# Moving the weight rounding to an even rhythm, the packed scores one step later, and computing the router's logits with the router's weights held still in four column groups

## The chip, the cores and the metric

The kernel runs on one core of one Trainium2 chip. The metric is the device time of one execution in microseconds; the time before is the median of three runs. The engines are named as the profile names them: PE is TensorE (PEld its weight loads), ACT is ScalarE, DVE is VectorE, POOL is GpSimd, SP is SyncE, which issues nearly all of the DMAs.

## The reference

```python
# packed attention, 8 batches x 8 heads, 576 tokens, 32 packed queries, head size 64
p_packed = sm_attn(p, k, v)
out = sm_attn(q, p_packed, p_packed)
# a dense layer on the 4608 tokens of width 512, inner width 2048
h = x @ w_in; x = (h * sigmoid(h)) @ w_out
# a router with 8 experts, one expert per token, inner width 1024
logits = x @ w_gate; e_idx = argmax(logits); gate_w = softmax(logits)[e_idx]
eom = sigmoid(x @ w_output_gate)[e_idx]
out = gate_w * eom * (relu(x @ w1[e_idx]) @ w2[e_idx])
```

## The kernel before

Batches 0 to 7 run one after the other in the function batch. Each has 16 steps f, one for each 128 of the 2048 inner columns of the dense layer. A step issues on PE, in this order: mm1 (12 matmuls of 288 columns, into the two banks of the PSUM tile h, of which there is one), whatever the schedule names for position 0 of the step, mm2 of two steps earlier (12 matmuls of 512 columns into four accumulators acc0 to acc3), and what the schedule names for position 1. On ACT and DVE it issues the gate: ACT's tanh reads h (L658), DVE's product reads h (L659), ACT rounds to the high half ghi (L664), DVE subtracts for the low half glo (L669); the last 64 tokens have halves of their own (gl). The next mm1 may start when L659 is done with h.

The order of the instructions on each engine is the program's (the schedule is written out by hand); semaphores come from the tile framework, which follows who uses which tile.

Work that rides along in these steps:

- The attention of the next batch, s1 to s9. s1(0) and s1(1) are the scores of the packed queries with the two halves k0 and k1 of the keys. They write the shared PSUM tile of pool ps_a (there is one, too); DVE takes the maximum (L535) and ACT copies the scores to e (L536). After s1(1), two exponentials (L542) run on ACT in the next step, and s2(0), at position 1 of step 4, transposes their first half.
- step_m at position 0 of the even steps: the fused query weights of two of the next steps, 16 matmuls of 64x32 tiles into ps_a.
- The rows of the batch before. At step 1 the last mm2 of batch b-1 is issued; ACT then moves the four accumulators out (evac, L711). Where b is even, a fifth accumulator, accL, follows at once in the place of acc3 (48 matmuls). row_t transposes two blocks of 128 tokens at steps 3 and 7, row_logits takes their logits at steps 5 and 9 (where b is even a single fifth block follows at 11 and 13). finish finds the experts, place counts and scatters the tokens' numbers into the tables perm (POOL, indirect DMA) at step 11 or 15, and the rows go to memory as xr (SP).
- split_slot, in batches 1 to 6: ACT rounds a raw piece of the expert weights (512 KB) to a tile shi, of which there are two (L478), DVE subtracts (L479), the next step stores both parts (ws, L466 and L467), and the slot itself issues the load of a later piece. There are 64 pieces; slots are the steps with f % 3 < 2, ahead of mm2 in the program. SP works its list in order, so a DMA that has to wait holds up those behind it.

row_logits holds 128 tokens as weights for each of four slices of 128 features and moves the 8 router columns past them: 8 matmuls for a pair of blocks, each of two fp32 instructions. In the last batch's tail (last_rows) the same is done between blocks of the accL matmuls. After batch 7 the experts run in tiles of 128 tokens.

Of the kernel before, what the change touches and what calls it, by code (L numbers as in the profile page):

```python
# [8 lines left out]
F32 = mybir.dt.float32  # L9
F32R = mybir.dt.float32r  # L10
# [3 lines left out]
ALU = mybir.AluOpType  # L14
# [5 lines left out]
B, H, S, D = 8, 8, 576, 64  # L20
# [3 lines left out]
NF = FF // 128  # L24
E8 = 8
# [5 lines left out]
XW = DM + 1  # L31
SCALE = 1.0 / 8.0

C_ID, C_E, C_OFF, C_LT, C_J, C_END = 0, 128, 136, 144, 208, 209
HS = S // 2
EARLY = 3
NSTATIC = NBLK + 2
# [3 lines left out]
def constants():  # L41
    p = np.arange(128)
    c = np.zeros((128, C_END), np.float32)
    c[:, C_ID:C_ID + 128] = np.eye(128)
    e = np.arange(E8)
    c[:, C_E:C_E + E8] = e
    c[:, C_OFF:C_OFF + E8] = (e - E8) * CAP
    c[:, C_LT:C_LT + E8 * E8] = (e[None, :] < e[:, None]).reshape(1, -1)
    c[:, C_J] = p
    k = np.full((128, 256), 0x3F80, np.uint16)  # L50
    k[:, :128] *= p[:, None] < p[None, :]
    t = np.stack([block_tokens(i) for i in range(NBLK)], axis=1).astype(np.int32)
    t[:, np.arange(NBLK) % NPERM > 0] -= NTOK
    return {"cst": c, "cstk": k, "cstt": t}
# [25 lines left out]
class Kernel:  # L80
# [12 lines left out]
    def run(self):  # L93
        tc, nc = self.tc, self.nc
# [21 lines left out]
        self.flip = False  # L116
        self.ppt, self.m, self.g, self.loads = {}, {}, {}, {}
        self.graws = []
        self.wgt = cp.tile([128, 4, E8], F32, name="wgt")
        self.tok = self.rt.tile([128, NBLK], I32, name="tok")  # L120
        self.w_in = self.pin.tile([128, 4, FF], F32, name="w_in")
        self.a1 = [self.pa.tile([128, 5, 128], F32, name="a1t")]
# [96 lines left out]
    def last_rows(self):  # L219
        b = B - 1  # L220
        self.mm2(b, NF - 2)
        hi, lo = self.g.pop((b, NF - 1))
        g = self.rows_group(b, range(4))
        for j in (3, 0, 1, 2):
            self.mm2_block(self.acc[j], hi[:, j * 128:j * 128 + 128], lo[:, j * 128:j * 128 + 128], NF - 1, False, True)
        for j in (3, 0, 1, 2):
            self.evac(g, j, self.acc[j])
        acc = self.ps_acc.tile([128, 512], F32, tag="acc3", name="accL")
        side = {2: lambda: self.row_t(g, 3, 0), 5: lambda: self.row_logits(g, 3, 0),
                6: lambda: self.row_t(g, 1, 2), 9: lambda: self.row_logits(g, 1, 2),  # L230
                12: lambda: self.place(g)}
        for ff in range(NF):
            self.mm2_block(acc, self.gl[0][:, ff, :], self.gl[1][:, ff, :], ff, ff == 0, ff == NF - 1)
            if ff in side:
                side[ff]()
            run(self.late)
        self.group_l = self.rows_group(b, [4], g)
        self.evac(self.group_l, 4, acc)
# [17 lines left out]
            g["t"][j] = t  # L256

    def row_logits(self, g, *js):
        ps = self.ps_a.tile([128, 2, 512], F32, tag="a", name="ps_rl")
        for n, j in enumerate(js):  # L260
            for k in range(4):
                self.nc.tensor.matmul(ps[:, 0, n * E8:n * E8 + E8], g["t"][j][:, k * 128:k * 128 + 128], self.wgt[:, k, :],
                                      start=(k == 0), stop=(k == 3))
        for n, j in enumerate(js):
            g["left"] -= 1
            self.nc.vector.tensor_copy(out=g["lg"][:, g["at"][j], :], in_=ps[:, 0, n * E8:n * E8 + E8])
        if not g["left"]:
            self.finish(g)

# [64 lines left out]
    def batch(self, b, hook=None):  # L334
        sched = self.extra_steps(b)
        for f in range(NF):
            s = b * NF + f
            self.split_store()
            self.mm1(b, f)
            self.fill(b, 1, True)  # L340
            self.act(b, f)
            run(sched.get((f, 0), []))
            self.split_hi(b, f)
            self.split_lo(b, f)
            wait = f < 2 and b % 2 == 0 and b > 0
            self.graws = [*self.graws[-1:], self.graw]
            if not wait:
                self.split_left(b, f, self.graw)
            run(self.late)
            if 0 < b < B - 1 and f % 3 < 2:  # L350
                self.split_slot()
            self.fill(b, 2 if f < 2 else 1)
            if s > 1:
                self.mm2(*divmod(s - 2, NF))
            if wait and f == 1:
                for i in range(2):
                    self.split_left(b, i, self.graws[i])
            run(sched.get((f, 1), []))
            if hook:
                hook(f)  # L360
            if b == 0 and f == 8:
                self.a2[1] = [self.p1.tile([128, 2, S], F32R, tag=f"a2_1{i}", name="a2") for i in range(2)]
            if b == 0 and f == 4:
                self.setup_late()
            if b == 0 and f == 0:
                t = self.rt.tile([128, 4, 512, 2], U32, tag="wg", name="stg4")
                for i in range(4):
                    self.f64_load(t[:, i], True)
            if b == 0 and f == 14:
                self.mid = self.rt.tile([128, E8 * DM], F32, tag="wg", name="mid")  # L370
                self.nc.sync.dma_start(self.wgt, self.i["wgt"])

    def fill(self, b, conv, defer=False):
        if b == 0:
# [2 lines left out]
    def extra_steps(self, b):  # L377
        sched = {}

        def at(f, pos, fn):  # L380
            sched.setdefault((f, pos), []).append(fn)

        if b + 1 < B:
            att = self.att_steps(b + 1)
            for f, pos, *step in ((0, 1, "s1", 0), (2, 1, "s1", 1), (4, 1, "s2", 0), (5, 1, "s3", 0), (6, 1, "s2", 1),
                                  (7, 1, "s3", 1), (8, 1, "s4"), (9, 1, "s5", 0), (10, 0, "s6", 0), (10, 1, "s7", 0),
                                  (11, 1, "s8", 0), (11, 1, "s9", 0), (12, 1, "s5", 1), (13, 0, "s6", 1), (13, 1, "s7", 1), (14, 1, "s8", 1), (14, 1, "s9", 1)):
                at(f, pos, att[tuple(step)])
            for f, what in ((0, "k1"), (2, "q0"), (5, "v1"), (9, "q1")):
                at(f, 1, lambda what=what: self.load_att(b + 1, what))  # L390
            at(14, 0, lambda: self.step_m(b + 1, 0))
        if b + 2 < B:
            for what in ("p", "k0", "v0"):
                at(13, 0, lambda what=what: self.load_att(b + 2, what))
        if b > 0:
            js = [(3, 0), (1, 2)] + ([(4,)] if b % 2 == 0 else [])
            for n, r in enumerate(js):
                at(4 * n + 3, 0, lambda r=r: self.row_t(self.group, *r))
                at(4 * n + 5, 0, lambda r=r: self.row_logits(self.group, *r))
            at(4 * len(js) + 3, 0, lambda: self.place(self.group))  # L400
        for c in range(1, 8):
            at(2 * c - 2 + (b == 0 and (c == 1 or c % 2 == 0)), 0, lambda c=c: self.step_m(b, c))
        return sched
# [65 lines left out]

    def split_slot(self):  # L470
        nc = self.nc
        if not self.split_raw:
            self.split_raw = [self.mid[:, k * 1024:k * 1024 + 1024] for k in (1, 2, 3)]
            self.split_raw += [self.stg.tile([128, 1024], F32, name="sw")]
        if len(self.split_loaded) == 2 or not self.split_jobs:
            for w, dst in self.split_loaded[:1]:
                hi = self.stg.tile([128, 1024], F32R, tag="shi", bufs=2, name="shi")
                nc.scalar.copy(out=hi, in_=w)  # L478
                nc.vector.tensor_tensor(out=w.bitcast(F32R), in0=w, in1=hi.bitcast(F32), op=ALU.subtract)  # L479
                self.split_done.append((w, hi, dst))  # L480
            self.split_loaded = self.split_loaded[1:]
        if self.split_jobs:
            which, e, k = self.split_jobs.pop(0)
            w = self.split_raw[self.split_n % 4]
            self.split_n += 1
            if which == 1:
                nc.sync.dma_start(w, self.i["w1"][e].rearrange("(k p) f -> p k f", p=128)[:, k, :])
                dst = self.ws1[e, k]
            else:
                nc.sync.dma_start(w.rearrange("p (k d) -> p k d", k=2),  # L490
                                  self.i["w2"][e].rearrange("(k p) d -> p k d", p=128)[:, 2 * k:2 * k + 2, :])
                dst = self.ws2[e, k]
            self.split_loaded.append((w, dst))


    def load_att(self, b, what, dst=None):
# [206 lines left out]
    def rows_group(self, b, js, rest=None):  # L703
# [1 line left out]
        n = len(js)  # L705
        return {"n": n, "left": n, "b": b, "js": js, "at": {j: k for k, j in enumerate(js)}, "t": {},
                "xr": rt.tile([128, 5, XW], F32, tag="xr", name="xr") if rest is None else rest["xr"][:, 4:5],
                "lg": rt.tile([128, 5, E8], F32, tag="lg", bufs=2, name="lg")}

    def evac(self, g, j, acc):  # L710
        self.nc.scalar.activation(out=g["xr"][:, g["at"][j], :DM], in_=acc, func=AF.Copy, scale=0.5)  # L711
# [323 lines left out]
```

## Time and profile before

| what | value |
|---|---|
| median of three runs | 1384.9 us (1384.56 to 1385.53) |
| the profiled execution | 1384.82 us, its span 1383.1 us |
| mean granted TensorE clock | 0.969 |
| PE busy | 1279.1 us, 92% |
| DVE, ACT, POOL busy | 652.3, 506.6, 172.8 us |
| DMA | 238.56 MB, mean 172 GB/s |

A busy share is a mean over stages with different limits. The clock is the share of 2.4 GHz that was granted; 0.5 is 1.2 GHz. An arrow in a row names what ended the idle time before an instruction.

### The profile page before, as it was taken

Reading aid. Unit: us, or ns where it says so; the run is one execution under the profiler, and the core shown is the slowest. Engines: PE = TensorE matmul, PEld = TensorE weight load, DVE = VectorE, ACT = ScalarE, POOL = GpSimd, SP = SyncE. Lnnn points to the kernel's source line nnn. Section 1 sums busy time; section 2 is a strip of 40 time slices with the busy share of each in tenths; the row PEclk is TensorE's granted clock in tenths of the full one; section 3 lists DMA queues with packets and bytes.
Section 4 is the critical chain, followed back from the end, with each engine's and each line's share of the span. In section 5 each row is a group of like instructions: output and inputs, shape, how many; then the busy total and the mean of one; then the engine's idle time right before and its main releaser. Section 6 shows DMA issues by size and latency. Waiting matters only on the chain. (4 is left out here: it accounts for less than half of the span.)

```text
span 1383.1 us, 24453 instructions
## 1 busy us (share of the span) xinstructions
PE 1279.1 (92%) x8414; PEld 1024.6 (74%) x8416; DVE 652.3 (47%) x1417; ACT 506.6 (37%) x980; POOL 172.8 (12%) x236
## 2 busy tenths in 40 slices
PE   6776999799799899899899999969999999999997
PEld 3555787687587687687687888748888888888886
DVE  6979558257557356657356644311222222222221
ACT  3323544354454354454354433212232222222222
POOL 0324101000101000101000111111122122112210
PEclk9899999999899999999999999989999999999999
DMA  8553259665977755987955317651555473822630
GB/s 293 195 171 109 79 203 172 236 234 201 198 251 171 237 192 194 253 246 161 246 190 185 100 31 151 108 124 47 191 191 199 156 269 109 293 63 70 222 137 22
DMA packets 110623, 238.56 MB, mean 172 GB/s; under 512 B 30753, under 2 KB 48929, under 8 KB 110498
## 3 DMA queue, kind: packets, MB, share of 16 engines
q1 hardware_dynamic: 103266, 217.46, 53.0%
q0 software_dynamic: 7232, 19.44, 4.1%
q8 instruction: 77, 1.26, 0.4%
q14 instruction: 48, 0.39, 0.1%
HBM read 401.91 MB, written 87.14 MB: 354 GB/s over the span
## 5 line engine op out<-in xcount | busy, mean ns | idle before, releaser
L700 PE MATMUL acc<-wo,ghi 128*128 128x512 f32 x1024 | 320.4, 394 | 0.0
L700 PEld LDWEIGHTS acc<-wo,ghi 128*128 128x128 f32 x1024 | 194.5, 190 | 38.7
L649 PE MATMUL ps_h<-a,m_hi 128*128 128x288 f32 x1024 | 213.7, 301 | 0.8 <-DVE a L615 0.8
L700 PE MATMUL acc<-wo,glo 128*128 128x512 f32 x512 | 212.5, 415 | 0.6 <-ACT xr L711 0.6
L992 PE MATMUL py<-queue_q_buf,hhi 128*128 x608 | 191.9, 397 | 0.0
L649 PE MATMUL ps_h<-a,m_lo 128*128 128x288 f32 x512 | 162.9, 318 | 24.0 <-DVE g L659 20.9
L964 PE MATMUL pu<-queue_q_buf,xhi 128*128 x560 | 175.9, 395 | 0.0
L978 DVE TENSOR_TENSOR hlo<-ph,hhi 128x512 fp32r<-128x512 f32 x76 | 49.0, 686 | 263.1 <-ACT hhi L977 152.7
L649 PEld LDWEIGHTS ps_h<-a,m_hi 128*128 128x128 f32 x1024 | 169.6, 194 | 2.6 <-DVE a L615 1.0
L659 DVE SCALAR_TENSOR_TENSOR g<-g,ps_h 128x576 f32<-128x576 f32 x128 | 96.1, 751 | 132.0 <-ACT g L658 131.6
L658 ACT ACTIVATE g<-ps_h 128x576 f32<-128x576 f32 x128 | 83.3, 651 | 157.8 <-PE ps_h L649 153.3
L649 PEld LDWEIGHTS ps_h<-a,m_lo 128*128 128x128 f32 x512 | 99.1, 194 | 51.2 <-DVE g L659 30.2
L992 PE MATMUL py<-queue_q_buf,hlo 128*128 x304 | 123.7, 407 | 13.4 <-DMA xix_p<-perm 13.4
L992 PEld LDWEIGHTS py<-queue_q_buf,hhi 128*128 128x128 f32 x608 | 115.4, 190 | 25.6
L700 PEld LDWEIGHTS acc<-wo,glo 128*128 128x128 f32 x512 | 97.4, 190 | 43.3 <-issue 25.0
L767 POOL DMA_INDIRECT perm<-tok,dsti x36 | 38.5, 1069 | 682.8 <-DVE dsti L764 649.6
L964 PEld LDWEIGHTS pu<-queue_q_buf,xhi 128*128 128x128 f32 x560 | 105.2, 188 | 23.8
L664 ACT CAST ghi<-g 128x512 fp32r<-128x512 f32 x128 | 79.3, 620 | 106.5 <-DVE g L659 104.4
L964 PE MATMUL pu<-queue_q_buf,xlo 128*128 x280 | 114.3, 408 | 0.2 <-ACT hs L966 0.2
L966 ACT ACTIVATE hs<-pu 128x512 f32<-128x512 f32 x76 | 45.4, 598 | 166.4 <-PE pu L964 158.1
L669 DVE TENSOR_TENSOR glo<-g,ghi 128x512 fp32r<-128x512 f32 x128 | 88.5, 691 | 31.4 <-ACT ghi L664 26.7
L997 POOL DMA_INDIRECT out<-y,xix x38 | 38.3, 1009 | 335.1 <-ACT y L995 330.2
(183 smaller groups left out, 1513.8 us busy)
## 6 DMA issues: line engine op xcount, KB each, us to landing
queue_q_buf<-ws SPq DMA_DIRECT2D x70, 4096.0 KB
ws<-shi SPq DMA_DIRECT2D x64, 512.0 KB
mid<-in_w SPq DMA_DIRECT2D x48, 512.0 KB
ws<-mid SPq DMA_DIRECT2D x48, 512.0 KB
att_v<-in_v SPq DMA_DIRECT2D x15, 640.0 KB
og<-in_wog SPq DMA_DIRECT2D x35, 256.0 KB
att_k<-in_k SPq DMA_DIRECT2D x15, 576.0 KB
xr<-xr SPq DMA_DIRECT2D x32, 256.5 KB
```

What stands on the lines that cost most here:

```text
L649: nc.tensor.matmul(ps[:, hf, :288], lw[:, qd, fs], rx[:, qd, ts], start=(i == 0), stop=(i == 5))
L658: nc.scalar.activation(out=g2, in_=ps[:, :, :288], func=AF.Tanh, scale=0.5)
L659: nc.vector.scalar_tensor_tensor(out=g2, in0=g2, scalar=1.0, in1=ps[:, :, :288], op0=ALU.add, op1=ALU.mult)
L664: self.nc.scalar.copy(out=hi, in_=self.graw[:, :512])
L669: self.nc.vector.tensor_tensor(out=lo, in0=self.graw[:, :512], in1=self.ghi.bitcast(F32), op=ALU.subtract)
L700: self.nc.tensor.matmul(acc, l, r, start=(first and i == 0), stop=(last and i == 2))
L767: nc.gpsimd.indirect_dma_start(out=self.perm[(i0 + r) % NPERM], out_offset=bass.IndirectOffsetOnAxis(ap=di[:, r:r + 1], axis=0), in_=self. ...
L964: nc.tensor.matmul(ps, l[:, ks], w[:, k, r, ns], start=(i == 0), stop=(i == 11))
L966: nc.scalar.activation(out=self.hs[j][:, n * 512:n * 512 + 512], in_=ps, func=AF.Relu)
L978: nc.vector.tensor_tensor(out=lo[:, n], in0=ps, in1=hi[:, n].bitcast(F32), op=ALU.subtract)
L992: nc.tensor.matmul(ps, l[:, k // 4, ks], w[:, k // 2, r, (k % 2) * DM:(k % 2) * DM + DM], start=(i == 0), stop=(i == 23))
L997: nc.gpsimd.indirect_dma_start(out=self.out, out_offset=bass.IndirectOffsetOnAxis(ap=ix[:, 0:1], axis=0), in_=y, in_offset=None, bounds_ch ...
```

## The change

Six edits: a slot is a step with (s - 16) % 3 < 2 where s counts through the batches, so the rhythm doesn't start anew in each batch; at step 1 the slot comes after mm2, the evacuation and accL; two pieces are loaded at the end of batch 0, so every slot rounds one piece and loads one; s1(1) and the load of q0 move from step 2 to step 3; a pair's logits are computed with 32 columns of router weights held still in one of four column groups, 128 tokens moving, into four partial results that ACT copies to SBUF, and one step later one matmul with a 0/1 matrix sums them and turns them back; lg has one buffer in place of two.

```diff
-C_ID, C_E, C_OFF, C_LT, C_J, C_END = 0, 128, 136, 144, 208, 209
+C_ID, C_E, C_OFF, C_LT, C_J, C_SEL, C_END = 0, 128, 136, 144, 208, 209, 225
+    n = np.arange(2 * E8)
+    c[:, C_SEL:] = (p[:, None] % 32 == n % E8) & (p[:, None] // 32 % 2 == n // E8)
...
-        side = {2: lambda: self.row_t(g, 3, 0), 5: lambda: self.row_logits(g, 3, 0),
-                6: lambda: self.row_t(g, 1, 2), 9: lambda: self.row_logits(g, 1, 2),
+        side = {2: lambda: self.row_t(g, 3, 0), 4: lambda: self.row_logits(g, 3, 0), 5: lambda: self.row_logits2(g, (3, 0)),
+                6: lambda: self.row_t(g, 1, 2), 8: lambda: self.row_logits(g, 1, 2), 9: lambda: self.row_logits2(g, (1, 2)),
...
     def row_logits(self, g, *js):
...
+        for k in (0, 2, 1, 3):
+            for n, j in enumerate(js):
+                c = 2 * (k // 2) + n
+                nc.tensor.matmul(ps[32 * c:32 * c + 32, 0, :128], self.wgt[:, k * E8:k * E8 + 32], g["t"][j][:, k * 128:k * 128 + 128],
+                                 start=(k % 2 == 0), stop=(k % 2 == 1))
+        g["part"] = g["t"][js[1]][:, :128]
+        nc.scalar.copy(out=g["part"], in_=ps[:, 0, :128])
+
+    def row_logits2(self, g, js, h=None):
+        ps = (self.ps_a.tile([128, 2, 512], F32, tag="a", name="ps_rl") if h is None else h)[:, 0, 288:288 + 2 * E8]
+        self.nc.tensor.matmul(ps, g["part"], self.cst[:, C_SEL:C_SEL + 2 * E8], start=True, stop=True)
+        self.row_logits_out(g, ps, js)
...
-            if 0 < b < B - 1 and f % 3 < 2:
+            slot = 0 < b < B - 1 and (s - NF) % 3 < 2
+            if slot and f != 1:
                 self.split_slot()
             self.fill(b, 2 if f < 2 else 1)
             if s > 1:
                 self.mm2(*divmod(s - 2, NF))
+            if slot and f == 1:
+                self.split_slot()
...
+            if b == 0 and f == 15:
+                self.split_load()
+                self.split_load()
...
-            for f, pos, *step in ((0, 1, "s1", 0), (2, 1, "s1", 1), (4, 1, "s2", 0), (5, 1, "s3", 0), (6, 1, "s2", 1),
+            for f, pos, *step in ((0, 1, "s1", 0), (3, 1, "s1", 1), (4, 1, "s2", 0), (5, 1, "s3", 0), (6, 1, "s2", 1),
...
-            for f, what in ((0, "k1"), (2, "q0"), (5, "v1"), (9, "q1")):
+            for f, what in ((0, "k1"), (3, "q0"), (5, "v1"), (9, "q1")):
...
                 at(4 * n + 5, 0, lambda r=r: self.row_logits(self.group, *r))
+                if len(r) == 2:
+                    at(4 * n + 6, 0, lambda r=r: self.row_logits2(self.group, r, self.h))
...
     def split_slot(self):
         nc = self.nc
...
+        for w, dst in self.split_loaded[:1]:
+            hi = self.stg.tile([128, 1024], F32R, tag="shi", bufs=2, name="shi")
+            nc.scalar.copy(out=hi, in_=w)
+            nc.vector.tensor_tensor(out=w.bitcast(F32R), in0=w, in1=hi.bitcast(F32), op=ALU.subtract)
+            self.split_done.append((w, hi, dst))
+        self.split_loaded = self.split_loaded[1:]
+        self.split_load()
...
-                "lg": rt.tile([128, 5, E8], F32, tag="lg", bufs=2, name="lg")}
+                "lg": rt.tile([128, 5, E8], F32, tag="lg", name="lg")}
```

split_load is the loading half of the old split_slot, on its own. row_logits_out holds the two copies to lg on DVE and the call of finish. The router's tile wgt grows from 32 to 56 columns, zeroed first, since every group of 32 is read with the columns behind it.

## Rows read from the trace of the kernel before

**Rows 1.** The page's span and its PE, DVE and ACT totals.

```profile
span 1383.1 us, 24453 instructions
PE 1279.1 (92%) x8414; PEld 1024.6 (74%) x8416; DVE 652.3 (47%) x1417; ACT 506.6 (37%) x980; POOL 172.8 (12%) x236
```

**Rows 2.** Stretches: length, busy by engine (count), granted clock, DMA share, GB/s.

```profile
155.70:159.90 4.20, 4.20 (x30) 3.75 (x25) 1.67 (x3) 2.10 (x5) 0.00 (x0) 1.00 0.65 203
159.90:171.06 11.16, 11.16 (x90) 8.83 (x89) 6.19 (x13) 7.44 (x16) 0.00 (x0) 1.00 0.37 125
247.69:271.09 23.40, 17.38 (x79) 14.16 (x72) 4.57 (x5) 5.76 (x9) 0.00 (x0) 0.85 0.76 288
362.86:384.79 21.93, 13.86 (x89) 10.99 (x89) 7.50 (x14) 9.09 (x19) 0.96 (x1) 0.77 1.08 140
460.22:482.70 22.48, 17.46 (x79) 14.22 (x72) 4.57 (x5) 5.77 (x9) 0.00 (x0) 0.85 0.71 268
574.50:593.00 18.50, 13.70 (x88) 10.88 (x88) 7.51 (x14) 9.03 (x19) 0.96 (x1) 0.82 0.97 169
668.46:691.27 22.81, 17.07 (x79) 13.92 (x72) 4.57 (x5) 5.77 (x9) 0.00 (x0) 0.85 0.78 292
```

**Rows 3.** Waits of the execution: us in total, times, longest.

```profile
ACT e L536 <- DVE sm L535: 52.6, 15, 9.9
...
PE accL L700 <- ACT xr L711: 16.8, 3, 6.0
...
ACT shi L478 <- DMA ws<-shi: 15.0, 4, 4.7
...
PE ps_s L520 <- DMA att_k<-in_k: 13.8, 4, 7.8
```

**Rows 4.** Timeline of ACT from step 0 to 1 of batch 4.

```profile
462.67 1.05 ACT L478 CAST shi<-sw 128x1024 fp32r<-128x1024 f32 x1 [4.15 <-DMA ws<-shi]
...
465.74 0.64 ACT L536 COPY e<-ps_s 128x576 f32<-128x576 f32 x1 [2.02 <-DVE sm L535]
...
468.27 1.04 ACT L478 CAST shi<-mid 128x1024 fp32r<-128x1024 f32 x1
...
469.22 2.05 ACT L711 ACTIVATE xr<-acc 128x512 f32<-128x512 f32 x4
```

**Rows 5.** Timeline of step 5 of batch 7: start, length, engine, line.

```profile
799.89 1.88 PEld L262 LDWEIGHTS ps_rl<-wgt,mid 128*128 128x128 f32 x16
...
800.27 0.65 ACT L658 ACTIVATE g<-ps_h 128x576 f32<-128x576 f32 x1 [2.88 <-PE ps_h L649]
...
800.95 0.76 DVE L659 SCALAR_TENSOR_TENSOR g<-g,ps_h 128x576 f32<-128x576 f32 x1 [2.85 <-ACT g L658]
...
801.68 0.19 PEld L700 LDWEIGHTS acc<-wo,glo 128*128 128x128 f32 x1
```

**Rows 6.** Timeline of the weight loads around one step_m and one s3.

```profile
172.95 0.18 PEld L520 LDWEIGHTS ps_m<-w_in,ppt 64*32 64x32 f32 x16 [0.16 <-issue]
173.54 0.19 PEld L700 LDWEIGHTS acc<-wo,glo 128*128 128x128 f32 x1 [0.41 <-issue]
...
183.17 0.60 PEld L564 LDWEIGHTS ps_s<-att_v,a1t 128*32 128x32 f32 x40 [0.35 <-issue]
183.87 0.19 PEld L649 LDWEIGHTS ps_h<-a,m_lo 128*128 128x128 f32 x1
```

**Rows 7.** Timeline of ACT and PEld in steps 3 and 4 of batch 1.

```profile
170.05 0.77 ACT L542 ACTIVATE e<-e,sm 128x576 f32<-128x576 f32 x1
170.72 0.19 ACT L542 ACTIVATION_READ_ACCUMULATOR e<-e,sm 128x1 f32 x1
...
175.09 0.24 ACT L676 CAST gl<-g 128x64 fp32r<-128x64 f32 x1
...
176.17 0.67 PEld L550 LDWEIGHTS ps_s<-cst,e 128*128 128x128 f32 x5
```

**Rows 8.** Stretches in batch 0 and at the end of batch 1, columns as in rows 2.

```profile
84.00:90.00 6.00, 4.44 (x37) 3.12 (x36) 5.63 (x8) 2.75 (x7) 2.10 (x2) 1.00 0.65 231
51.00:57.90 6.90, 4.39 (x29) 2.84 (x28) 6.70 (x11) 2.94 (x6) 1.39 (x2) 0.75 0.65 223
226.00:244.00 18.00, 16.90 (x118) 13.60 (x117) 12.86 (x22) 7.88 (x15) 0.76 (x1) 1.00 1.08 75
```

More of the change, by code (lines that the diff above doesn't have):

```diff
@@ L118, in run @@
         self.graws = []
-        self.wgt = cp.tile([128, 4, E8], F32, name="wgt")
+        self.wgt = cp.tile([128, 3 * E8 + 32], F32, name="wgt")
         self.tok = self.rt.tile([128, NBLK], I32, name="tok")
@@ L258, in row_logits, with row_logits_out @@
     def row_logits(self, g, *js):
+        nc = self.nc
         ps = self.ps_a.tile([128, 2, 512], F32, tag="a", name="ps_rl")
-        for n, j in enumerate(js):
+        if len(js) == 1:
             for k in range(4):
-                self.nc.tensor.matmul(ps[:, 0, n * E8:n * E8 + E8], g["t"][j][:, k * 128:k * 128 + 128], self.wgt[:, k, :],
-                                      start=(k == 0), stop=(k == 3))
+                nc.tensor.matmul(ps[:, 0, :E8], g["t"][js[0]][:, k * 128:k * 128 + 128], self.wgt[:, k * E8:k * E8 + E8], start=(k == 0), stop=(k == 3))
+            self.row_logits_out(g, ps[:, 0, :E8], js)
+            return
+        for k in (0, 2, 1, 3):
[9 more added lines that the diff above has]
+        self.row_logits_out(g, ps, js)
+    def row_logits_out(self, g, ps, js):
         for n, j in enumerate(js):
             g["left"] -= 1
-            self.nc.vector.tensor_copy(out=g["lg"][:, g["at"][j], :], in_=ps[:, 0, n * E8:n * E8 + E8])
+            self.nc.vector.tensor_copy(out=g["lg"][:, g["at"][j], :], in_=ps[:, n * E8:n * E8 + E8])
         if not g["left"]:
@@ L370, in batch @@
                 self.mid = self.rt.tile([128, E8 * DM], F32, tag="wg", name="mid")
-                self.nc.sync.dma_start(self.wgt, self.i["wgt"])
+                self.nc.vector.memset(self.wgt, 0.0)
+                self.nc.sync.dma_start(self.wgt[:, :4 * E8].rearrange("p (k e) -> p k e", e=E8), self.i["wgt"])
+            if b == 0 and f == 15:
+                self.split_load()
+                self.split_load()
     def fill(self, b, conv, defer=False):
@@ L471, in split_slot @@
         nc = self.nc
[L472 to L493, printed above, removed]
+        for w, dst in self.split_loaded[:1]:
[3 more added lines that the diff above has]
+            self.split_done.append((w, hi, dst))
@@ new lines, in split_slot, with split_load @@
+        self.split_loaded = self.split_loaded[1:]
+        self.split_load()
+    def split_load(self):
+        nc = self.nc
+        if not self.split_jobs:
+            return
+        which, e, k = self.split_jobs.pop(0)
+        n = self.split_n
+        self.split_n += 1
+        if n < 3:
+            self.split_raw.append(self.mid[:, (n + 1) * 1024:(n + 2) * 1024])
+        elif n == 3:
+            self.split_raw.append(self.stg.tile([128, 1024], F32, name="sw"))
+        w = self.split_raw[n % 4]
+        if which == 1:
+            nc.sync.dma_start(w, self.i["w1"][e].rearrange("(k p) f -> p k f", p=128)[:, k, :])
+            dst = self.ws1[e, k]
+        else:
+            nc.sync.dma_start(w.rearrange("p (k d) -> p k d", k=2),
+                              self.i["w2"][e].rearrange("(k p) d -> p k d", p=128)[:, 2 * k:2 * k + 2, :])
+            dst = self.ws2[e, k]
+        self.split_loaded.append((w, dst))
```

## The prediction

> **What bounds the kernel now.** I read the totals first: PE is busy 1279.1 of 1383.1 us, DVE and ACT less than half of it [rows 1]. So time goes where PE's list gets shorter, or where PE stands still. Next the windows, one for each step of the loop. A plain step (mm1 and mm2, nothing else) takes 4.20 us with PE busy throughout, at the full clock; the two steps 2 and 3 of batch 1 take 11.16 us, again without a hole [rows 2]. That is the floor. Against it stand the first steps of batches 2 to 6. Step 1 of batches 2, 4 and 6 takes 23.40, 22.48 and 22.81 us. Its floor is 4.20 us plus accL: the plain step moves 12 x 288 + 12 x 512 = 9600 columns in 4.20 us, so the 48 x 512 = 24576 of accL need 10.75; together 14.95. The excess is 8.45, 7.53 and 7.86 us. Steps 2 and 3 of batches 3 and 5 take 21.93 and 18.50 us against 11.16: 10.77 and 7.34 us. In all 41.95 us, and in each of these stretches the granted clock is below 1, 0.77 to 0.85 [rows 2]: PE pays the hole, and then runs part of the work behind it at 1.2 GHz.
>
> What ends the holes, by the list of waits: in even batches accL waits for ACT's evacuation (16.8 us in three), in odd ones the scores wait for the keys att_k (13.8 us in four) [rows 3]. The timeline of ACT says why the evacuation is late in batch 4: the rounding of step 0 stood 4.15 us behind a store of shi, then came the copy of the scores, the gate of step 1 and the rounding of step 1 (1.04 us), and only then the evacuation at 469.22 [rows 4]. The store is late since the DMA engines, though booked full, moved only 75 GB/s in such a stretch [rows 8].
>
> **The boundaries, part by part.** My sum is made against the profiled execution, 1384.8 us, within 0.1 us of the median.
>
> Odd batches: s1(1) goes one step later and so has about 5 us more (the steps 2 and 3 of batch 1 are 11.16 us together, a plain step is 4.20 [rows 2]). In batch 5 the hole was the shorter one: the stretch has 4.80 us without PE busy [rows 2], so it closes, and its half clock with it: 7.3 us gained. In batch 3 8.07 us of the stretch are without PE, the wait itself up to 7.8 us [rows 2, 3]; some 2.7 us remain if the keys land when they did. They may land a little earlier, since no slot is at step 0 of batch 3 any more and one load of 512 KB less stands ahead of them. I take 8.5 of the 10.8 us, with 5 and 10.8 as ends.
>
> Even batches: at step 1 no rounding stands ahead of the evacuation, which is 1.04 us [rows 4]. In batch 6 the new rhythm has no slot at step 0 either, so the whole chain from the late store to the evacuation is gone; it rounded a step earlier, with PE two steps of mm2 ahead of need. I take 7.5 us of 7.86. In batch 4 the slots before it are 10, 11, 13, 14 in place of 9, 10, 12, 13 and 15: slot 0 still needs the buffer of slot 13, but the store of slot 12 that went ahead of it is now that of slot 11, a step earlier. I halve the 4.15 us wait and take 3.5 of 7.53 us, ends 0 and 7.5. In batch 2 the slots are the old ones; only the 1.04 us is sure, ends -2 (the rows xr, below) and 3.
>
> Sum of the boundaries: 7.3 + 8.5 + 7.5 + 3.5 + 1.0 = 27.8 us gained; by the ends 17 to 37.
>
> **The logits.** Before: from the first weight load of a pair to the next of mm2, 799.89 to 801.68, 1.79 us for 16 loads of 128 columns, 0.112 each [rows 5]. The new form does not stand in the trace; its nearest rows are the tile stages: 16 instructions of 64x32 tiles with 256 columns hold PE 0.59 us, 40 of 128x32 with 64 columns 0.70 [rows 6]. In one column group the new form moves 4 x 128 = 512 columns, those two 2 x 256 = 512 and 10 x 64 = 640. I take 0.70 (the shape is that of s3), bounds 0.59 and 0.9 with the holes of 0.4 that the profile shows around such stages. It saves 1.09 us a pair. ACT's copy of 128x128 falls between tanh and ghi, where ACT waits for DVE's product; the nearest rows are 0.24 us for 64 columns (L676) and 0.65 for the 576 of tanh [rows 5, 7]. I cost it at nothing: the cover is the 0.76 us of L659, and without it 0.3 us would fall on ghi, which mm2 needs two steps later.
>
> The second matmul is two more such loads: 0.23 us. But where it stands decides. It writes columns 288 to 303 of h, right behind mm1, while tanh and the product of the same step still have to read h. Does the program make PE wait for them, though the columns differ? The trace has a like case: the copy of the scores on ACT needs nothing of DVE's maximum, both only read ps_s, and yet ACT waited for DVE 15 times, 52.6 us [rows 3], 2.02 us of it in [rows 4]. So two engines' uses of one PSUM tile are put in order here even where nothing is overwritten. I take it that PE waits until L659 is done: from 799.89, when PE had mm1 issued, to 800.95 + 0.76 = 801.71, that is 1.82 us, and some 0.08 for the semaphore: 1.9 us [rows 5]. Queued behind it on PE are step_m and mm2, so nothing covers it; ACT's rounding of step_m slides with them, DVE has the time.
>
> The Trainium skill speaks for this wait too: "PSUM — Partial Sum Buffer", section "PSUM bank collisions raise a hardware error", has it that two engines' accesses must be kept apart by bank and quadrant, not by address, so distinct columns of one bank are no licence. By that rule the 14 sums in h cost what I have just taken; without it they would cost the loads alone.
>
> Per pair in the steps: -1.09 + 0.23 + 1.9 = +1.04 us; 14 pairs (batches 1 to 7, two each): +14.6. In the tail the sum has a ps_a tile of its own, between blocks of accL: -0.86 for each of two pairs, -1.7. While PE stands at step 10, DVE catches up on what it lagged by at step 11 of the odd batches; I give 2 us back for that (all waits of this kind are a small part of the 1383.1 - 1279.1 us without PE). Logits in all: +10.9; by the bounds +7 to +16, and -14 if PE doesn't wait.
>
> **The rest.** The exponentials now run in step 4, behind gl, which ended at 175.33; the first takes until its sum is read, 0.86 us, so 176.2, and s2(0) loads at 176.17 [rows 7]: 0.2 us lost a batch, 1.2 for six; if the tile e is taken whole, the second one counts too and it is 1.0 us a batch, 6 in all. Nothing hides it, PE waits in its place. The rows xr of odd batches go out a step later (finish follows the second matmul): SP's list is then held one step later by the gate's weight, its loads and stores of before that step leave sooner. I cost that at nothing: the same bytes pass, in another order. If the 1 MB of xr (4 x 256.5 KB) does come to stand ahead of the store that slot 0 needs, that is 3.6 us at the 288 GB/s of batch 2's stretch [rows 2], in each of batches 2 and 4. The two loads at the end of batch 0 and the zeroed wgt fall into idle queues: nothing. Batch 0's s1(1) at step 3 meets the same busy DVE as at step 2: 0, at most 3 either way.
>
> Sum: 1384.8 - 27.8 + 10.9 + 1.2 = 1369.1, with 1 us for what I have not seen: **1370**.
>
> **The rivals.**
> - *No wait in h.* Then 14 x 1.9 = 27 us less: 1343. For it: the columns differ. Against: the 15 waits of two mere readers [rows 3].
> - *All boundaries close.* 41.95 in place of 27.8: 1356. For it: each needs only 2 to 4 us less of a wait; against: batch 2's slots are unchanged.
> - *DMA takes it back.* The scatter's stretch [rows 8] now meets the rows xr, batches 2 and 4 gain nothing and batch 3 only 5: 1378.
> - *The clock falls at the new waits: slower.* A hole of 2.51 us (6.90 less 4.39) was followed by half clock, mean 0.75 over 6.9 us; one of 1.56 us (6.00 less 4.44) left it at 1.00 [rows 8]. The new waits are 1.9 us, between the two. A fall is 3.45 us at 1.2 GHz, 1.7 us of work lost; 14 of them 24 us: 1394. It decides from nine falls on.
> - *The holes at the boundaries stay*, since the next transfer in line is as late; only logits and exponentials count: 1397.
>
> **How the numbers follow.** Forecast 0.42, with a range of its own of 1361 to 1379; no wait 0.07; all close 0.14; DMA 0.15; clock 0.13; holes stay 0.09. Below 1354 lies the case without a wait, above 1391 the last and about half of the clock's: 2 in 10 in all. 0.2% is 2.8 us, about what a measurement of this kernel can tell from no change. Faster: the first four but for a part of the DMA case, 0.72; same: its edge and that of the clock's, 0.08; slower 0.20.
>
> **What would show it.** On PE at steps 6 and 10 a wait of about 1.8 us ended by DVE L659, none if the first rival holds. At steps 5 and 9 a stage of 0.7 us in place of 1.8. No wait of accL for ACT in batch 6, a shorter one in batch 4, one of 5 us still in batch 2. A wait for att_k of up to 3 us in batch 3, none in batch 5. The clock at 1.00 around steps 6 and 10. I am wrong if the stores of shi still hold ACT ahead of an evacuation, or if the new wait is not there.

## The result, and the profile after

The changed kernel takes 1398.15 us (median of four runs, 1395.31 to 1412.48), the kernel before 1384.73 beside it (1384.46 to 1385.53): ratio 1.0113, 95% interval 1.008 to 1.0146. It is slower, by 1.1%. The profiled execution took 1399.96 us at a mean granted clock of 0.962. Its totals, to be held against [rows 1]:

```profile
span 1398.2 us, 24546 instructions
PE 1278.2 (91%) x8446; PEld 1015.6 (73%) x8448; DVE 653.0 (47%) x1418; ACT 507.8 (36%) x996; POOL 174.0 (12%) x236
```

PE has as much to do as before; the time without work on PE grew from 104.0 to 120.0 us. The windows, columns as in [rows 2], show where: steps 5 and 6 of batch 1, step 6 of batch 2, then the boundaries (steps 0 and 1 of batch 2, 2 to 4 of batch 3, 0 and 1 of batch 4, 2 to 4 of batch 5, 0 and 1 of batch 6).

```profile
175.74:181.74 6.00, 6.00 (x83) 4.77 (x80) 3.05 (x6) 3.22 (x8) 0.00 (x0) 1.00 0.84 330
181.74:191.00 9.26, 7.67 (x54) 6.02 (x48) 3.93 (x8) 2.84 (x5) 0.00 (x0) 0.82 0.57 203
295.76:303.42 7.66, 6.07 (x53) 4.86 (x48) 3.82 (x9) 2.85 (x5) 0.00 (x0) 1.00 0.82 285
241.58:251.36 9.78, 6.09 (x59) 4.17 (x57) 3.94 (x6) 3.44 (x6) 0.00 (x0) 1.00 1.01 254
251.36:272.77 21.41, 18.62 (x80) 15.36 (x73) 3.41 (x5) 4.81 (x8) 0.00 (x0) 0.84 0.60 219
364.96:391.18 26.22, 19.43 (x134) 14.92 (x133) 10.59 (x19) 11.98 (x24) 0.95 (x1) 0.80 1.02 171
462.70:488.19 25.49, 22.86 (x127) 17.91 (x128) 6.21 (x9) 7.32 (x13) 0.00 (x0) 0.93 0.73 240
582.13:606.40 24.27, 19.33 (x134) 14.88 (x133) 11.16 (x21) 12.15 (x25) 1.16 (x1) 0.86 0.98 143
677.44:700.31 22.87, 22.87 (x127) 17.82 (x128) 6.21 (x9) 7.32 (x13) 0.00 (x0) 0.93 0.70 270
```

The same windows of the kernel before:

```profile
176.84:183.87 7.03, 7.03 (x83) 6.15 (x81) 2.77 (x8) 2.16 (x5) 0.00 (x0) 1.00 0.52 209
183.87:189.59 5.72, 5.72 (x52) 4.55 (x46) 3.00 (x6) 2.91 (x5) 0.00 (x0) 1.00 0.63 206
...
362.82:390.52 27.70, 19.63 (x133) 15.60 (x133) 11.47 (x20) 13.40 (x26) 0.96 (x1) 0.82 1.04 179
454.24:482.73 28.49, 23.47 (x130) 18.38 (x128) 8.58 (x11) 9.28 (x15) 0.00 (x0) 0.88 0.75 280
574.52:598.81 24.29, 19.49 (x134) 15.49 (x134) 11.47 (x20) 13.40 (x26) 0.96 (x1) 0.86 0.94 190
662.53:691.32 28.79, 23.05 (x130) 18.09 (x129) 8.58 (x11) 9.38 (x15) 0.00 (x0) 0.88 0.83 282
```

**Logits.** Step 5 is 1.0 us shorter, as forecast. Step 6 is 1.9 us longer in batch 2 and 3.5 in batch 1. The timeline of batch 1 has the reason, the wait that the prediction named, and the window behind it the half clock:

```profile
184.39 0.76 DVE L692 SCALAR_TENSOR_TENSOR g<-g,ps_h 128x576 f32<-128x576 f32 x1 [2.22 <-ACT g L691]
185.20 0.30 PEld L278 LDWEIGHTS ps_h<-cst,mid 128*128 128x128 f32 x2 [1.82 <-DVE g L692]
185.20 0.40 PE L278 MATMUL ps_h<-cst,mid 128*128 128x16 f32 x2 [1.59 <-DVE g L692]
```
```profile
186.60:190.00 3.40, 3.40 (x10) 2.65 (x9) 2.65 (x4) 1.89 (x4) 0.00 (x0) 0.50 0.21 84
```

All 14 waits of this kind are 1.59 us long on PE (list of waits, below); behind 8 of them the granted clock fell to 0.50, behind 6 it stayed at 1.00. Steps 5 to 11 of batches 1 to 7 together are 19.3 us longer than before.

**Boundaries.** The five windows sum to 130.0 us against 139.8: 9.8 gained where 27.8 was forecast. And step 15 of batches 3 and 5 went from 4.37 us to 8.36 and 8.67, 8.3 lost: there ACT stands in a slot until a store of shi is done, the next tanh is late (it starts at 461.10), and PE waits for the product (ACT, then PE, at the end of batch 3):

```profile
457.50 1.05 ACT L501 CAST shi<-sw 128x1024 fp32r<-128x1024 f32 x1 [2.40 <-DMA ws<-shi]
```
```profile
462.70 0.40 PE L682 MATMUL ps_h<-a,m_lo 128*128 128x288 f32 x1 [3.77 <-DVE g L692]
```

So 1384.8 + 19.3 - 9.8 + 8.3 = 1402.6; the other steps give back the 2.6 us to the profiled 1400.0. The list of waits (us in total, times, longest) shows ACT's rounding waiting twice as long for stores as in [rows 3]:

```profile
ACT shi L501 <- DMA ws<-shi: 33.7, 8, 8.3
...
PE ps_h L278 <- DVE g L692: 22.2, 14, 1.6
```

### The profile page after: what moved, and what is told of

It reads as the page before. It is cut to its first block, busy times and chain, and to the rows that moved or that the text cites. A ratio compares the mean times of both kernels' runs of the same rounds, so it can differ in the third digit from the quotient of the medians.

```text
span 1398.2 us, 24546 instructions
## 1 busy us (share of the span) xinstructions
PE 1278.2 (91%) x8446; PEld 1015.6 (73%) x8448; DVE 653.0 (47%) x1418; ACT 507.8 (36%) x996; POOL 174.0 (12%) x236
## 5 line engine op out<-in xcount | busy, mean ns | idle before, releaser
L733 PE MATMUL acc<-wo,ghi 128*128 128x512 f32 x1024 | 329.9, 404 | 0.0
L733 PEld LDWEIGHTS acc<-wo,ghi 128*128 128x128 f32 x1024 | 201.0, 196 | 41.0
L733 PE MATMUL acc<-wo,glo 128*128 128x512 f32 x512 | 218.8, 427 | 0.0
L1025 PE MATMUL py<-queue_q_buf,hlo 128*128 x304 | 123.9, 408 | 14.6 <-DMA queue_q_buf<-ws 14.6
L733 PEld LDWEIGHTS acc<-wo,glo 128*128 128x128 f32 x512 | 100.5, 196 | 47.6 <-issue 28.6
L502 DVE TENSOR_TENSOR mid<-mid,shi 128x1024 fp32r<-128x1024 f32 x48 | 58.8, 1225 | 62.8 <-ACT shi L501 62.8
```

The source lines that it names most:

```text
L733: self.nc.tensor.matmul(acc, l, r, start=(first and i == 0), stop=(last and i == 2))
L1025: nc.tensor.matmul(ps, l[:, k // 4, ks], w[:, k // 2, r, (k % 2) * DM:(k % 2) * DM + DM], start=(i == 0), stop=(i == 23))
```

## The experiments

"Before" below is the kernel before on the same chip. The rows come from four sessions, each with its own "before": the result; old logits to sum late; scores alone and no scatters; the last four. The median of "before" was 1384.7, 1387.9, 1388.3 and 1388.7 us in them, so a difference in us between rows of different sessions is good to some 4 us, and the ratios compare better. The boundary sum is the sum of the five windows above, read in the same way.

| kernel | us | ratio to before (95%) | boundary sum |
|---|---|---|---|
| before | 1384.7 to 1388.7 | | 139.8 |
| after | 1398.15 | 1.0113 (1.008 to 1.0146) | 130.0 |
| old logits | 1377.88 | 0.9932 (0.9883 to 0.9982) | 133.7 |
| logits alone | 1400.74 | 1.0095 (1.0065 to 1.0124) | 145.4 |
| filled wait | 1405.4 | 1.0126 (1.0084 to 1.0169) | 148.6 |
| sum late | 1378.05 | 0.9931 (0.9897 to 0.9965) | 137.8 |
| scores alone | 1386.45 | 0.9972 (0.9943 to 1.0001) | 142.5 |
| no scatters | 1362.59 | 0.9806 (0.9783 to 0.9829) | 98.2 |
| no scatters, filled | 1349.86 | 0.9721 (0.9698 to 0.9744) | 98.1 |
| no scatters, old logits | 1346.47 | 0.9703 (0.9679 to 0.9726) | 98.1 |
| old logits, scatters at step 7 | 1354.69 | 0.9762 (0.9734 to 0.979) | 98.2 |
| before, scatters at step 7 | **1349.78** | 0.9735 (0.9704 to 0.9767) | 100.8 |

**Old logits.** The changed kernel with row_logits as before.

```diff
-        side = {..., 4: lambda: self.row_logits(g, 3, 0), 5: lambda: self.row_logits2(g, (3, 0)), ...
+        side = {..., 5: lambda: self.row_logits(g, 3, 0), ...
-                if len(r) == 2:
-                    at(4 * n + 6, 0, lambda r=r: self.row_logits2(self.group, r, self.h))
```

> The changed kernel with the logits as they were before: the even rhythm, the later slot of step 1, the two early loads and the later scores alone. Theory A (the holes at the batch boundaries are set by when the DMA engines get through the stretch after the scatter; another rhythm only changes which instruction stands in it): the holes stay nearly as they are in the changed kernel, and only the logits' cost goes, which the steps 5, 6, 9, 10 and 11 of the two traces put at 19 us, so about 1379. Rival B (the boundaries would have closed as predicted, and it is the logits that spoil them, by sending the rows xr a step later and stretching the steps): 1357. Rival C (the new rhythm and the later scores are worth nothing or harm): 1385 or more.

1377.88 us, near theory A: the logits cost the changed kernel 20.3 us (25 by the two ratios), and the rhythm with the scores gained 10 of the forecast 27. The even batches came as forecast: windows 30.12, 22.96 and 21.36 us against 30.52, 28.49 and 28.79 before, 13.4 gained (forecast 12.0). The odd ones got worse, 33.03 and 26.25 against 27.70 and 24.29, where 15.8 was to be gained. In batch 3 PE waits for the keys:

```profile
386.56 1.22 PE L535 MATMUL ps_s<-att_k,att_p 64*32 64x288 f32 x16 [13.71 <-DMA att_k<-in_k]
```

**Logits alone.** The kernel before with the logits of the change.

> The kernel before with the new logits alone, old rhythm and old scores. By the step times of the changed kernel the two-part logits cost 19 us, of it some 13 us by eight falls of the clock behind the new waits: about 1404, and the boundaries as before. By the prediction's sum (waits of 1.9 us, no fall of the clock): 1396. If the boundaries suffer from the later rows xr as rival B has it: 1410 or more.

1400.74 us, 12.8 more than before, between the first two expectations. The clock falls five times at steps 6 and 10; steps 5 to 11 are 14.6 us longer in the profiled execution, and the boundary sum is 5.6 us larger.

**Filled wait.** The changed kernel with eight matmuls of zeros into ps_a ahead of the sum, so that PE isn't idle while it waits.

```diff
+        if h is not None:
+            ps_w = self.ps_a.tile([128, 2, 512], F32, tag="a", name="ps_w")
+            for _ in range(8):
+                self.nc.tensor.matmul(ps_w[:, 0, :], self.zero[:, :128], self.zero, start=True, stop=True)
```

> The changed kernel with eight matmuls of zeros (512 columns each, result unused) in the place where PE waits for L692 at steps 6 and 10, so that PE is as late but not idle. If the eight falls of the clock come from these waits and cost 1.6 us each: none of them is left, about 1385. If the falls come from elsewhere or cost nothing: no change, 1398.

1405.4 us. The falls at steps 6 and 10 are gone (every step 6 of batches 1 to 6 takes 7.66 to 7.68 us), so they came from these waits, and yet no time was gained: the ratio, 1.0126, can't be told from the 1.0113 of the changed kernel, as in the second expectation but not for its reason. The boundary sum grew by 18.6: what PE gained, it waited for later. PE was not what set the time there.

**Sum late.** The changed kernel, the sum taken from behind mm1 to behind three of the four blocks of mm2, where DVE is done with h.

```diff
-                    at(4 * n + 6, 0, lambda r=r: self.row_logits2(self.group, r, self.h))
+                    at(4 * n + 6, 0, lambda r=r: self.sum_later(r))   # runs in mm2 when j == 3
```

> The changed kernel with the second matmul of the logits between the third and the fourth block of mm2 in the same step, where L692 has long been done: no wait and no fall of the clock behind it. If PE time is all that counts: 14 x 1.9 + 13 = 40 us less, about 1358. Theory A (the boundaries wait for DMA, which does not get faster): a part of it comes back as longer holes, 1365 to 1378, with no fall of the clock left at steps 6 and 10.

1378.05 us, at the upper end of theory A. Step 6 falls from 7.66 or 9.25 to 6.67 or 5.95 us, so the wait was the order of readers in h. At step 10 the next mm1 then waits up to 2.75 us for copies of lg queued on DVE, and behind three of these waits the clock falls; the boundary sum grew by 7.8.

**Scores alone.** The kernel before with s1(1) and the load of q0 at step 3.

```diff
-            for f, pos, *step in ((0, 1, "s1", 0), (2, 1, "s1", 1), ...
+            for f, pos, *step in ((0, 1, "s1", 0), (3, 1, "s1", 1), ...
-            for f, what in ((0, "k1"), (2, "q0"), ...
+            for f, what in ((0, "k1"), (3, "q0"), ...
```

> The kernel before with only the second scores and the load of q0 moved from step 2 to step 3. The prediction's sum for the odd batches: 15.8 us less, 1371, with the holes of batches 3 and 5 shrunk by a step's 5 us to 2.7 and 0. Theory A with nothing else changed ahead of the keys: the same, since the keys land when they did. If the load of the keys moves with the scores or with the clock: less than 5 us gained, 1380 or more.

1386.45 us, no change. The scores of batch 3 now run without a wait, so the keys were there in time. But ACT's rounding of step 3 stands 6.41 us behind a store of shi, the copy of the scores stands behind the rounding, and step_m of step 4 needs the PSUM tile that this copy frees (PE, ACT, PE):

```profile
377.92 0.71 PE L520 MATMUL ps_s<-att_k,att_p 64*32 64x288 f32 x16
383.13 1.04 ACT L478 CAST shi<-mid 128x1024 fp32r<-128x1024 f32 x1 [6.41 <-DMA ws<-shi]
386.82 1.11 PE L520 MATMUL ps_m<-w_in,ppt 64*32 64x256 f32 x16 [6.40 <-ACT e L536]
```

In batch 5 it is the same with 3.09 us on ACT and 3.06 us on PE.

**No scatters.** By now the holes ended at a transfer, the keys or a store of shi, whichever instruction met it. The DMA view of the kernel before for 221 to 250 us, its rates in 40 slices of 0.725 us, has what precedes the boundary of batch 2:

```profile
DMA  9999998599999608569999898994859949999999
GB/s 254 305 407 390 441 429 312 176 328 153 23 62 28 23 11 57 28 102 209 226 95 22 13 10 8 24 23 8 40 54 73 66 154 412 433 377 427 396 424 407
...
q0 software_dynamic: 128, 0.00, 0.4%
...
perm<-tok,dsti POOLq DMA_INDIRECT x4
```

For some 16 us (slices 11 to 32) the engines are booked nearly full and move 8 to 226 GB/s, mostly under 70; behind it, after one slice of 154, come 377 to 433. Just before it begins, at 228.25 us, POOL issued the scatters of the rows' numbers (L767, from 221.5 to 226.8 us). This kernel is the changed one without the scatters of batches 0 to 4 (22 of 36), its tables perm filled with zeros, so the experts work on other rows.

```diff
+            if g["b"] < 5:
+                return
             for r in range(n):
                 nc.gpsimd.indirect_dma_start(out=self.perm[...], ...
```

> The changed kernel without the scatters of the rows of batches 0 to 4 (the indirect DMAs of L800 that would run in batches 1 to 5; the tables then hold zeros in their place, so the experts get token 0 for these rows, and their output is not the reference's). Theory A (the scatter's stretch of slow DMA makes the holes at the boundaries): the holes of batches 2 to 6, 28.5 us of PE without work in the changed kernel's trace, and the falls of the clock behind them, some 8 us more, go for the most part: 1362 to 1370. Rival D (the rounding's own loads and stores, 1.5 MB a slot, or SP's order are what is late): the holes stay, 1390 or more.

1362.59 us, within theory A, 35.6 below the changed kernel (some 42 by the two ratios). No boundary has a hole left, and the boundary sum is 31.8 less. The same DMA view:

```profile
DMA  4000005999998999999999999999999300005999
GB/s 198 0 11 0 0 0 190 379 379 280 102 96 229 311 285 401 424 390 287 303 281 309 401 381 372 418 412 424 412 390 362 122 3 0 23 0 215 395 413 350
```

**Later scatter**, twice: the old-logits kernel and the kernel before, with the scatters written to step 4 of the next batch.

> The changed kernel with the old logits, and with the scatters of the rows of batches 0 to 4 issued in step 4 of the next batch in place of step 11 or 15. Theory A: the boundaries are free of the slow stretch, the holes before accL and the second scores go; steps 4 to 7 may wait for the stores of shi instead, but nothing like accL hangs on them: 1355 to 1370. Rival D: as with the old logits alone, 1378. Rival E (the stretch costs its time wherever it lies, since ACT stands in a slot there too): 1375 to 1385.

> The kernel before with nothing but the scatters of the rows of batches 0 to 4 moved to step 4 of the next batch. Theory A: most of the 42 us of excess at the boundaries goes, 1350 to 1365. Rival D: no change, 1387. Rival E: 1380 to 1390, the holes now around steps 5 to 8.

1375.9 us (0.9891, 0.9844 to 0.9937) and 1384.58 us (0.9977, 0.9952 to 1.0002). These tell nothing of a later scatter: only POOL's instructions moved in the program, POOL has nothing else in its list there, and so it still issued them at 221.5 us, as soon as DVE's dsti was there. They are repeats of the kernels they were made from, and so show the spread: the boundary sums are 131.4 (133.7 in the first) and 141.5 (139.8), and a single window differs by up to 3.3 us (batch 5 with the old logits: 22.99 and 26.25). Less than that in one window is no effect.

**Scatters at step 7.** The same two with the cast to dsti moved as well, so that POOL has to wait.

```diff
+            def scatter():
+                v.tensor_copy(out=di[:, :n], in_=d[:, :n, 0])
+                for r in range(n):
+                    nc.gpsimd.indirect_dma_start(...)
+            if g["b"] < 5:
+                self.scat.append(scatter)        # run at f == 7 of the next batch
```

> The changed kernel with the old logits (1377.9 us), and with the cast of the destinations and the scatters of the rows of batches 0 to 4 taken from the end of a batch to step 7 of the next one, behind the boundary. Theory A (the boundary's holes come from the DMA stretch that the scatters make slow just as the next batch's keys and scores are read): the boundary steps fall to about what they are without scatters, and the 12 to 18 us that a scatter slows land in steps that read ahead: 1345 to 1365 us. Rival E (the slow stretch costs its time wherever it lies, since the expert weights are then late by as much): 1373 to 1380 us, with holes at steps 8 to 12 or at the shared blocks' stores instead.

> The kernel before with the scatters of the rows of batches 0 to 4 taken to step 7 of the next batch, and nothing else. Theory A: the holes at its boundaries (batch 2 step 1 at 23.4 us, batch 4 step 1 at 22.5, batch 6 step 1 at 22.8, against 15.4 where nothing waits) close without any of the change's edits: 1350 to 1368 us. Rival E: 1380 to 1390 us.

1354.69 and 1349.78 us, as theory A had it. The kernel before gains 39.0 us from that move alone, and its boundary sum falls by 39.0. Its windows of steps 0 and 1 of batch 2 (both), 2 to 4 of batch 3 and 0 and 1 of batch 4:

```profile
239.98:245.93 5.95, 5.95 (x58) 4.16 (x57) 4.71 (x7) 4.46 (x7) 0.00 (x0) 1.00 0.59 195
245.93:262.26 16.33, 15.39 (x80) 12.70 (x73) 3.88 (x5) 4.82 (x8) 0.00 (x0) 1.00 0.63 224
...
358.69:375.64 16.95, 16.95 (x134) 13.47 (x133) 11.35 (x20) 12.81 (x25) 0.00 (x0) 1.00 0.91 337
439.16:461.50 22.34, 21.40 (x130) 16.86 (x128) 8.58 (x11) 9.28 (x15) 0.00 (x0) 1.00 0.71 261
```

The slow stretch moved along with the scatters, which POOL now issues from 297.25 to 303.2 us. The DMA view of the same kernel for 297 to 318 us, in slices of 0.525 us:

```profile
DMA  0299999689300000020300000000994024954294
GB/s 0 86 406 382 429 406 289 148 343 398 112 0 0 1 0 0 0 16 0 31 0 0 0 0 0 0 0 0 37 31 2 2 7 114 48 33 31 18 33 48
```

SP issues nothing from 299.2 to 310.49 us; what it issues then moves 2 to 114 GB/s in a slice, where the transfers before moved up to 429. No boundary lies there; what it costs is a few us (under "Open" below).

**No scatters, filled; no scatters, old logits.** The price of the logits where no hole takes time back; both leave out what "no scatters" leaves out.

> The changed kernel without the scatters (1362.6 us) and with eight matmuls of zeros ahead of the sum, so that TensorE isn't idle while the sum's step waits. With the boundaries closed, nothing should give the time back any longer. If the half clock behind the waits costs 1.6 us each time, some nine of them: 1348 us. Rival (DMA or VectorE gives it back as it did with the scatters there): 1360 to 1363 us.

> The changed kernel without the scatters (1362.6 us) and with the old logits: the price of the new logits where no boundary's hole takes part. By the step lengths of the changed kernel (steps 5 and 9 one us shorter, steps 6 and 10 longer by 1.9 or 3.5 us) the logits cost 19 us: 1343 us. Rival (the pairs' columns are worth what the prediction's sum had, 10.9 us): 1352 us.

1349.86 and 1346.47 us. Nine falls at steps 6 and 10 cost 1362.6 - 1349.9 = 12.7 us, 1.4 each; the wait with all else of the new logits costs 3.4; together 16.1. The lengths of steps 5 to 12 in the three profiled executions give 14.0, 6.3 and 20.3 (that of the old logits is 3.6 us below its median), so the price is 16 to 20 us, most of it by the clock.

## Why the prediction was wrong

It forecast 1370 us, faster; it is 1398, slower. Point by point:

- *What bounds the kernel:* right that the boundaries hold some 42 us of holes; moving the scatters got 39.0 back. The row with the slow stretch stood there [rows 8], and one rival calls it the scatter's. The prediction read it only as the reason why a store is late; it didn't ask what else the stretch makes late, or what makes the stretch.
- *Odd batches, 15.8 us gained, measured 1.5: the step that failed.* The sum let the keys alone end these holes, "if the keys land when they did", and put nothing on ACT's rounding in steps 2 and 3, which can wait for a store of shi in the same slow stretch. "Scores alone" shows the second half of it: the scores had their five us and found the keys there, and a store of shi made the hole instead. In the changed kernel the new rhythm has a slot at step 2 of batch 3. ACT stands in it for 8.27 us, its and DVE's copies of row_t come late, and the scores, which queue for the same PSUM tile, wait for them (ACT, then PE):

```profile
378.82 1.04 ACT L501 CAST shi<-sw 128x1024 fp32r<-128x1024 f32 x1 [8.27 <-DMA ws<-shi]
382.45 1.22 PE L553 MATMUL ps_s<-att_k,att_p 64*32 64x288 f32 x16 [6.79 <-DVE mid L257]
```

  The first half failed too. In batch 5 the keys end a wait of 4.94 us, 19.5 us after SP issued them, where it was 13.5 before; with the old logits they end the 13.71 us in batch 3. There SP's list had changed. Before, at the start of batch 3, behind the rows xr:

```profile
353.50 0.59 SPq L490 DMA_DIRECT2D mid<-in_w  x1
354.19 0.45 SPq L466 DMA_DIRECT2D ws<-shi  x1
355.68 0.34 SPq L467 DMA_DIRECT2D ws<-sw  x1
356.07 0.48 SPq L490 DMA_DIRECT2D mid<-in_w  x1
359.55 0.60 SPq L509 DMA_DIRECT2D att_k<-in_k  x1
```

and after (the order with the old logits is the same):

```profile
354.23 0.62 SPq L523 DMA_DIRECT2D mid<-in_w  x1
354.95 0.44 SPq L493 DMA_DIRECT2D ws<-shi  x1
355.49 0.38 SPq L494 DMA_DIRECT2D ws<-mid  x1
355.91 1.18 SPq L523 DMA_DIRECT2D sw<-in_w  x1
358.58 0.33 SPq L493 DMA_DIRECT2D ws<-shi  x1
359.49 0.33 SPq L494 DMA_DIRECT2D ws<-mid  x1
361.13 0.60 SPq L542 DMA_DIRECT2D att_k<-in_k  x1
```

  The slot that now falls on step 14 stores its pair one step later, so 1 MB more (358.58, 359.49) is ahead of the keys, in a stretch that moves 171 GB/s (windows after): by an estimate 6.1 us for 1.05 MB. The prediction had counted a load of 512 KB less. The list isn't the whole cause: in batch 5 its order is that of before, and the keys were late there as well. What made them late in batch 5 stays open.
- *Even batches, 12.0 us:* right in sum and place with the old logits (0.4, 5.5 and 7.4 us for 1.0, 3.5 and 7.5). With the new logits 8.3 us are left: the holes move again (25.49 us in batch 4, half clock in batch 6 behind the hole of step 15).
- *Step 15* was not in the sum: 8.3 us in batches 3 and 5. The slots' wait for stores is 5.3 of it; the other 3.0 are there without scatters too (5.86 us a step).
- *The wait in h:* right, 1.59 us on PE (1.82 on its weight load) for the forecast 1.9, in all 14 places. By the page "PSUM — Partial Sum Buffer" of the Trainium skill, section "PSUM bank collisions raise a hardware error", accesses are to be kept apart by bank and quadrant, not by address. The trace agrees with 14 waits for a reader of other columns; they come from the program's semaphores, and no run goes without them. The wait goes once the sum stands behind that reader ("sum late").
- *The clock at the new waits,* a rival at 0.13: it came in 8 of 14 places. The prediction put the point from which it decides at nine falls of 1.7 us; measured, 1.4 to 1.6 each. The logits stood at 10.9 us in the sum, and steps 5 to 11 grew by 19.3; eight falls of 1.6 are 12.7 of that. Without falls they would have cost less than forecast, since DVE's lag gave back 6.1 us at step 11 where 2 was taken.
- *Exponentials, 1.2 us:* nothing; steps 2 to 4 take 16.98 us against 16.95 where no hole is.
- *Rhythm and late scores where nothing is late:* old logits with the scatters moved is 4.9 us slower by the medians than the kernel before with them moved. They treated a symptom; step 1 of the even batches is 0.92 to 0.99 us shorter, but steps 12 to 15 of batches 3 and 6 are 2.1 us longer, and step 8 of batches 2 and 5 is 3.5 us longer.
- *The last rival, 1397 us,* is near the time by luck: it had the boundaries unchanged, where 9.8 us were gained, and 10.9 us for the logits, where 19.3 were lost.

**Open.** With the scatters at step 7 a few us are still lost near them, steps 10 and 11 of batch 2 taking 8.65 and 7.09 us where batch 4 has 5.05 and 5.76. PE's own list gives no partner for it (the weight load of mm2 at 316.81 comes 2.87 us late, and the profile has "issue" as its reason). What it waited for was not settled, nor why 6 of 14 equal waits left the clock alone. Spreading the scatters over several steps, and the new logits with a late sum once the scatters are out of the way, were not tried.

## What to carry to other kernels

A hole that ends at a transfer is closed at the transfer: look at the DMA rate in slices of about a microsecond ahead of it, and where the engines are booked but move a tenth of their rate, find what was issued just before that began, and move it. Moving the consumer by a step, or filling PE's waits, only moved the holes here: the next transfer of the same stretch ended them. An edit to a slot's step moves its stores in the issuing queue too: write that queue out, before and after, for the transfers that end the holes. And a new wait on PE is priced with and without a fall of the clock behind it.

## What the runs showed of the hardware

- Four scatters of 128 numbers of 4 bytes each (0.4% of the DMA engines' time on their own queue, in the stretch shown) go with some 16 us in which the other queue's transfers keep the engines booked and move mostly under 70 GB/s. The Trainium skill's page "DMA: Bandwidth & Descriptors", section "Issuing engines are not separate DMA queues", has DMAs of all issuers interleave on the same engines. The trace agrees: POOL's scatters hold up SP's transfers. It is 35.6 us for 22 scatters taken out (some 42 by the ratios), 1.6 to 1.9 each, and the stretch came along when the scatters were moved to 297 us. Why so small a write does it, no run shows.
- Of 14 waits of 1.59 us, each behind mm1 and in the same place of a step, eight were followed by 1.2 GHz and six by 2.4. Matmuls of zeros in the wait kept the clock at 2.4 GHz at all 14.
